# Squares into two buffers in turn, an order re-drawn for each short stretch, products strictly in order

## The chip, the cores and the metric

One Trainium2 chip, of which the kernel uses one core. The metric is the device time of one execution in microseconds (us): 1184.61 us, the median of three runs (1183.17 to 1184.68). The profile is a further execution, which took 1182.92 us.

## The reference, cut to what matters

`x` has 4 batches of 12608 tokens of 128 numbers; `inducing` has 32 points.

```
scale = 1/sqrt(128)
mab(q, kv): a = softmax(scale * q @ kv.T);  return a @ kv
h = mab(inducing, x)            # per batch: 32 points look at 12608 tokens ("p1")
x = mab(x, h)                   # each token looks at the 32 points       ("p2")
h = x @ w_in                    # 128 -> 1024
e = exp(h - max(h));  sm = e / sum(e)
solu = h * sm
ln = (solu - mean(solu)) / sqrt(var(solu) + 1e-6) * g_ln
out = ln @ w_out                # 1024 -> 128
```

All of it is fp32. The variance needs the sum of the squares of each row of 1024; only that sum is used, the squares themselves are not.

## The kernel before, in words

Tokens go in tiles of 128 rows, 99 to a batch, 396 in all; four tiles are a group, 25 groups to a batch. `p1` (L598) and `combine` (L903) make the 32 points of a batch, `p2` (L949) the weights of its tokens; both run ahead of the tiles that need them. The bulk is one pipeline per tile:

- `main` (L1198), `mm1` (L1219), tensor engine (PE): `h` of one tile, 128x1024, into PSUM (line L1233).
- `soft` (L1266), vector engine (DVE): scales it and takes its extreme (L1275); scalar engine (ACT): exp, with the sum of the row read out behind it (L1286); GpSimd (POOL): `e = h * e` (L1290).
- `square` (L1299), ACT: squares `e` with the sum of the row (L1301). The squares are written to one buffer, `sq` (L320), which nothing reads; the sum goes to `G["qe"]`.
- DVE again: a transpose of `e` in 32x32 blocks into the group's buffer `vt` (L1317), of which there are three.
- `products` (L1455), PE: when the four tiles of a group are turned, 32 steps of 32-row products for each half of the array (`w` = 0, 1), L1473. They are put on a list `stream[w]`, from which `beats` (L1146) takes one step at a time: beside a tile's `mm1`, beside turns of `p1` and `p2`, or alone (`driver`, L1174).
- `evacuate` (L1491) copies three groups' products out of PSUM by ACT or DVE (L1501); `finish` (L1513) works out the variances with small steps that go between ACT and POOL (L1526 to L1540) and scales the rows (L1547 on POOL, L1551 on ACT); `stored` (L1556) sends them out on the queue of SP.

The order of instructions on each engine is fixed when the program is built, by `Planner.run` (L237). It keeps a clock for each engine, gives every operation the price written beside it (1208 for L1275, 1133 for L1286, 2330 for L1290, 1040 for L1301, 1163 for L1317, in ns) and a delay from engine to engine (`AFTER`, L95), and takes, on the engine that is free first, the operation of the lowest priority number among those that are ready within a slack (400 ns on ACT, 100 on DVE and POOL, L85):

```
limit = max(clock[eng], first[1]) + self.slack[eng]
pick = min(
    (o for o in self.ops if o[0].eng == eng and o[1] <= limit),
    key=lambda o: (o[2][1] if o[0].prio is None else o[0].prio, o[3]),
)
```

Priorities count in tiles: an operation of tile t has t plus an offset, -8 for the exp, -4 for POOL's multiply and for the square, +2 for L1275, +12 for the transpose (L76 to L83). DMA issues are operations of the engine SP and are picked in the same way.

The chip itself keeps the order and waits by semaphores for what an instruction reads and overwrites. The plan doesn't price a wait between two squares; the build does put one there, as both write `sq`.

Of the kernel before, what the change touches and what calls it, by code (L numbers as in the profile page):

```python
# [10 lines left out]
BF16 = mybir.dt.bfloat16  # L11
U32 = mybir.dt.uint32
I32 = mybir.dt.int32
AF = mybir.ActivationFunctionType
# [5 lines left out]
P = 128  # L20
C = 128
M = 32
FF = 1024
# [7 lines left out]
JB = FF // M  # L31
# [7 lines left out]
NR_POOL = 0  # L39
OS_LATE = 2000  # L40
SLOTS = 3
PIECE = 4
TOKENS = 4
TURN_ON = 90
# [37 lines left out]
PR_SQ = -4  # L82
# [59 lines left out]
class Planner:  # L142
# [94 lines left out]
    def run(self):  # L237
        clock = self.clock
        while self.ops:
            first = min(self.ops, key=lambda o: (max(clock[o[0].eng], o[1]), o[3]))  # L240
            eng = first[0].eng
            limit = max(clock[eng], first[1]) + self.slack[eng]
            pick = min(
                (o for o in self.ops if o[0].eng == eng and o[1] <= limit),
                key=lambda o: (o[2][1] if o[0].prio is None else o[0].prio, o[3]),
            )
            self.ops = [o for o in self.ops if o[3] != pick[3]]
            op, ready, task = pick[:3]
            start = max(clock[eng], ready)
            if eng == "PE" and start - clock[eng] > FILL:  # L250
                self._fill(start - SPARE)
            self.now = start
            op.fn()
            end = start + (self._pe(start, op.cost) if eng == "PE" else op.cost)
            clock[eng] = end
            if eng == "SP":
                end = self.data = max(end + DMA_LAG, self.data) + op.moves / DMA_RATE
            done = Done(eng, end)
            self._step(task, done)
        assert not self.blocked, "the plan is stuck"  # L260
# [3 lines left out]
def set_attention_then_solu_kernel(ctx: ExitStack, tc: tile.TileContext, x, inducing, w_in, w_out, g_ln, out):  # L264
    nc = tc.nc
    NB, N, _ = x.shape
    scale = 1.0 / float(C) ** 0.5
# [24 lines left out]
    plan = Planner(SLACK)  # L292
    spawn, give = plan.spawn, plan.give

    def buf(shape, name, dtype=F32, where=None):
        return (where or const).tile(shape, dtype, name=name)

    def bufs(n, shape, name, dtype=F32):
        return [buf(shape, f"{name}{i}", dtype) for i in range(n)]
# [17 lines left out]
    where = bank_pool.__enter__()  # L317
    bank_e = [buf([P, 512], f"bank_e{i}", where=where) for i in range(8)]
    hn_b = bufs(3, [P, FF], "hn")
    sq = buf([P, FF], "sq", BF16)  # L320

    eu_b = buf([P, EUS, FF], "eu")
    xT_b = buf([C, PG, P], "xT")
# [781 lines left out]
    order, fins = [], []  # L1105
# [18 lines left out]
    for b in range(NB):  # L1124
        for js in fins[b]:
            js = list(js)
            while js:
# [2 lines left out]
                    slot_of[b, j] = (i, j == same[-1])  # L1130
                js = js[len(same) :]

    stream = [[], []]
    flow = {"idle": Event(), "left": 2 * NB * NG - 2, "half": False, "took": 0}

# [38 lines left out]
    def driver():  # L1174

        while flow["left"]:
            mine = [p for q in stream for p in q if p["j"] < JB]
            if not mine:
                flow["idle"] = Event()
                yield flow["idle"]  # L1180
                continue
            op = Op("PE", BEAT * JC, None, Done("PE", min(p["ready"] for p in mine)), prio=min(p["prio"] for p in mine))

            def step():
                beats(JC)
                op.cost = flow["took"]

            op.fn = step
            d = yield op
            closing(d)  # L1190
# [7 lines left out]
    def main():  # L1198
        t = 0
        for b in range(NB):  # L1200
            for j in order[b]:
                left = list(range(ff_groups[j][1]))
                spawn(open_group(b, j), t)
                while left:
                    for item in starts.get(t, ()):
                        spawn(*item)
                    near = left[:WINDOW_TILES]
                    rel = []
                    for s in near:
                        d = yield aT_ready[(b, ff_groups[j][0] + s)]  # L1210
                        rel += d
                    d = yield hw_ready[b]
                    rel += d
                    _, turn = yield TURN
                    hp, hrel = yield H.at(t + H_LAST)
                    op = Op("PE", 4 * BEAT, None, rel, hrel, prio=t - 50)
                    chosen = []

                    def mm1():  # L1219
                        def slot(s):  # L1220
                            return part_of[b, ff_groups[j][0] + s][1]

                        s = min(near, key=lambda s: (load(slot(s) % 2), s))
                        chosen.append(s)
                        ka, i = part_of[b, ff_groups[j][0] + s]
                        aT, hs = aT_of[(b, ka)]["aT"][0], hT[b][1]
                        r = i % 2 * 2

                        def whole(c):
                            for k in range(2 if c == 0 else 0):  # L1230
                                rows = slice((r + k) * M, (r + k + 1) * M)
                                cols = slice(k * 512, (k + 1) * 512)
                                nc.tensor.matmul(hp[:, cols], lhsT=aT[rows, i // 2, :], rhs=hs[rows, cols], start=True, stop=True)  # L1233

                        beats(4, (1 - i % 2,), whole)
                        op.cost = flow["took"]

                    op.fn = mm1
                    d = yield op
                    closing(d)  # L1240
                    s = chosen[0]
                    left.remove(s)
                    if not left and j == order[b][-1]:
                        give(HW, hT[b], d)
                    spawn(soft(t, b, j, s, hp, d), t)
                    t += 1
# [19 lines left out]
    def soft(t, b, j, s, hp, d):  # L1266
        G = grp[(b, j)]
        ka, i = part_of[b, ff_groups[j][0] + s]
        A = aT_of[(b, ka)]
        hn, rel = yield HN  # L1270
        nm, mrel = yield NM
        rn = A["aT"][1][:, i : i + 1]
        d = yield Op(
            "DVE", 1208,
            lambda: nc.vector.tensor_scalar(out=hn, in0=hp, scalar1=rn, scalar2=None, op0=ALU.mult, op1=ALU.min, accum_out=nm),  # L1275
            d, rel, mrel, prio=t + PR_HN,
        )
        give(H, hp, d)
        give(TURN, None, d)
        A["left"] -= 1  # L1280
        if not A["left"]:
            give(AT, A["aT"], d)
        srel = yield G["st"]
        e, rel = yield EU
        de = yield Op(
            "ACT", 1133, lambda: nc.scalar.activation(e, hn, AF.Exp, bias=nm, scale=-1.0, accum_out=G["qe"][:, s, 1:2]), d, rel, srel,  # L1286
            prio=t + PR_EX,
        )
        give(NM, nm, de)
        d = yield Op("POOL", 2330, lambda: nc.gpsimd.tensor_tensor(out=e, in0=hn, in1=e, op=ALU.mult), de, prio=t + PR_MU)  # L1290
        give(HN, hn, d)
        left = []

        def over(d):
            left.append(d)
            if len(left) == 2:
                give(EU, e, *left)

        def square():  # L1299
            ds = yield Op(  # L1300
                "ACT", 1040, lambda: nc.scalar.activation(sq, e, AF.Square, scale=1.0 / 32.0, accum_out=G["qe"][:, s, 0:1]), d,  # L1301
                prio=t + PR_SQ,
            )
            G["squared"].append(ds)
            over(ds)
            if (b, j) != final and len(G["squared"]) == ff_groups[j][1]:
                yield from floor(b, j)

        spawn(square(), t)
        n = ff_groups[j][1]  # L1310
        rel = yield G["vt"]
        if (b, j) == final:
            yield from straight(t, b, j, s, e, d, rel, over)
            return
        dt = yield Op(
            "DVE", 1163,
            lambda: nc.vector.transpose(  # L1317
                out=G["vtb"][:, : n * FF].rearrange("p (j s t) -> p j s t", j=M, s=n)[:, :, s, :],
                in_=e.rearrange("p (a f) -> p a f", f=M),
            ),  # L1320
            d, rel, prio=t + PR_TU,
        )
        over(dt)
        G["turned"].append(dt)
        if len(G["turned"]) == n:
            for w in range(2):
                spawn(products(b, j, t, w), t)
# [127 lines left out]
    def products(b, j, t, w):  # L1455

        G = grp[(b, j)]
        n = ff_groups[j][1]
        rows = n * M
        yield PAIR[w].at(t)  # L1460
        slot, last = slot_of[b, j]
        if slot == 0:
# [2 lines left out]
        bank, rel, mine = held[w]  # L1465
# [16 lines left out]

        ready = max(d.end + AFTER[d.eng]["PE"] for a in (G["turned"], rel, wc_ready.after) for d in a if d is not None)
        stream[w].append(dict(j=0, emit=emit, ready=ready, close=close, prio=t + PR_G2))
        if not last:
            give(PAIR[w], None)
        idle = flow["idle"]
# [192 lines left out]
```

## Time and profile before

| | |
|---|---|
| median of three runs | 1184.61 us (1183.17 to 1184.68) |
| the profiled execution | 1182.92 us |
| its span, first to last instruction | 1181.1 us |
| mean granted clock of the tensor engine | 0.994 |
| busy: PE, ACT, DVE, POOL | 1151.1, 1102.6, 1074.8, 1065.6 us |

A row of instructions gives the start in us, the length in us, the engine, the line, the operation, what it writes and reads, and in brackets the idle time before it with what ended it. Busy times are unions: two instructions that overlap count once. The read of an accumulator (ACTIVATION_READ_ACCUMULATOR) is the tail of the instruction above it; the next instruction may start before the tail ends. Windows give busy us of each engine in a stretch with the number of its instructions, the granted clock of the tensor engine, the share of time that the DMA engines moved data, and GB/s. A PE that is busy need not be full: a product by one half of the array counts as busy.

### The profile page before, as it was taken

The page shows a single profiled execution, that of the slowest core. Times are in us where ns is not written, and L with a number is a line of the kernel's source. Part 1 is how long each engine was busy: PE and PEld are TensorE (multiplying, and loading weights), DVE is VectorE, ACT ScalarE, POOL GpSimd, SP SyncE. Part 2 cuts the span into 40 slices and gives each one's busy share as a digit, 9 for nine tenths or more (in the row PEclk, how much of TensorE's full clock was granted, in tenths as well). Part 3 has the DMA queues.
Part 4 walks back from the last instruction along what each step waited for, and adds up shares of the span by engine and source line. Part 5 has one row for each costly group of instructions (what it writes and reads, how often), then busy time and mean ns, then how long its engine had stood idle before and what let it go on. Part 6 is the DMA issues. An engine that isn't in the chain of part 4 may idle for free.

```text
span 1181.1 us, 68196 instructions
## 1 busy us (share of the span) xinstructions
PE 1151.1 (97%) x30636; PEld 1055.0 (89%) x30636; DVE 1074.8 (91%) x1639; ACT 1102.6 (93%) x2191; POOL 1065.6 (90%) x612
## 2 busy tenths in 40 slices
PE   9999999999999999999999999999999999999996
PEld 7669989998889898999899999999988999999996
DVE  6799989898999899999899998999999999999981
ACT  5699899999999999999999999999999999999994
POOL 3399799898999989899899998989999999999994
PEclk9989999999999999999999999999999999999999
DMA  9532342522143433331423433341313131220103
GB/s 340 230 124 76 111 121 71 155 73 49 41 119 86 141 111 107 96 104 33 120 66 94 121 107 120 102 127 45 101 40 84 40 79 34 67 64 5 49 5 87
DMA packets 166884, 110.62 MB, mean 94 GB/s; under 512 B 78112, under 2 KB 131776, under 8 KB 166464
## 3 DMA queue, kind: packets, MB, share of 16 engines
q1 hardware_dynamic: 166592, 106.27, 31.0%
q8 instruction: 239, 3.92, 1.4%
q14 instruction: 53, 0.43, 0.1%
HBM read 53.51 MB, written 52.17 MB: 89 GB/s over the span
## 4 chain that ended last, share of the span: by engine, by line
PE 45%; POOL 23%; ACT 20%; issue 7%; DVE 3%; DMA 2%; SPq 0%; ACTq 0%; POOLq 0%; DVEq 0%
PE h L1473 32%; POOL eu L1290 16%; ACT sq L1301 9%; ACT eu L1286 6%; PE h L1233 4%; POOL spare L1290 3%; POOL spare L1547 3%; ACT spare L1286 1%; ACT xT L666 1%; ACT spare L1501 1%; PE h L850 1%; PE h L655 1%; ACT a L1013 1%; PE bank_e L557 1%; DMA dl<-dd 1%
## 5 line engine op out<-in xcount | busy, mean ns | idle before, releaser
L1473 PEld LDWEIGHTS h<-wc,vt 32*128 32x128 f32 (+1 forms) x25344 | 954.3, 185 | 45.8 <-issue 13.3
L1473 PE MATMUL h<-wc,vt 32*128 32x129 f32 (+1 forms) x25344 | 983.5, 273 | 10.4 <-ACT spare L1501 3.1
L1290 POOL TENSOR_TENSOR eu<-hn,eu 128x1024 f32<-128x1024 f32 x198 | 466.8, 2377 | 28.7 <-ACT eu L1286 27.7
L1233 PE MATMUL h<-hs,aT 32*128 32x512 f32 x1584 | 419.6, 607 | 6.0 <-DVE spare L1275 2.6
L1317 DVE STREAM_TRANSPOSE vt<-eu 128x1024 f32<-128x1024 f32 x327 | 397.7, 1229 | 11.4 <-POOL eu L1290 10.7
L1301 ACT ACTIVATE sq<-eu 128x1024 bf16<-128x1024 f32 x330 | 346.4, 1050 | 11.3 <-POOL eu L1290 6.5
L1290 POOL TENSOR_TENSOR eu<-spare,eu 128x1024 f32<-128x1024 f32 x132 | 311.7, 2379 | 11.2 <-ACT eu L1286 11.1
L1275 DVE TENSOR_SCALAR_CACHE_REDUCE hn<-h,rn 128x1024 f32<-128x1024 f32 x198 | 248.7, 1260 | 20.6 <-PE h L1233 12.2
L1275 DVE TENSOR_SCALAR_CACHE_REDUCE spare<-h,rn 128x1024 f32<-128x1024 f32 x198 | 248.2, 1260 | 20.7 <-PE h L1233 10.0
L1286 ACT ACTIVATE eu<-hn,nm 128x1024 f32<-128x1024 f32 x198 | 225.4, 1139 | 2.9 <-DVE hn L1275 2.7
L1290 POOL TENSOR_TENSOR spare<-spare 128x1024 f32<-128x1024 f32 x66 | 156.9, 2377 | 12.2 <-ACT spare L1286 12.2
L1286 ACT ACTIVATE eu<-spare,nm 128x1024 f32<-128x1024 f32 x132 | 150.4, 1140 | 2.3 <-DVE vt L1317 1.3
L1233 PEld LDWEIGHTS h<-hs,aT 32*128 32x128 f32 x1584 | 124.6, 186 | 27.5 <-DVE spare L1275 8.1
L1317 DVE STREAM_TRANSPOSE vt<-spare 128x1024 f32<-128x1024 f32 x65 | 80.0, 1231 | 2.0 <-POOL spare L1290 1.8
L1547 POOL TENSOR_TENSOR spare<-spare,fin 128x512 f32<-128x512 f32 x79 | 79.8, 1041 | 1.6
L1301 ACT ACTIVATE sq<-spare 128x1024 bf16<-128x1024 f32 x66 | 69.3, 1050 | 6.9 <-POOL spare L1290 5.3
L1286 ACT ACTIVATE spare<-spare,nm 128x1024 f32<-128x1024 f32 x66 | 75.2, 1140 | 0.4 <-DVE spare L1275 0.4
L1301 ACT ACTIVATION_READ_ACCUMULATOR sq<-eu 128x1 f32 x330 | 62.6, 190 | 0.0
L655 PE MATMUL h<-ident,xn 32*128 32x32 f32 x1188 | 53.6, 227 | 0.1
L655 PEld LDWEIGHTS h<-ident,xn 32*128 32x128 f32 x1188 | 51.1, 141 | 1.1 <-issue 0.8
L1501 ACT COPY spare<-h 128x774 f32<-128x774 f32 (+3 forms) x66 | 42.5, 646 | 9.3 <-PE h L1473 7.0
L666 ACT COPY xT<-h 128x1024 f32<-128x1024 f32 (+2 forms) x42 | 37.8, 900 | 1.1 <-PE h L655 1.1
(189 smaller groups left out, 849.6 us busy)
## 6 DMA issues: line engine op xcount, KB each, us to landing
out_dram<-spare SPq DMA_DIRECT2D x95, 256.0 KB, 3.3
xT<-xd SPq DMA_DIRECT2D x93, 256.0 KB, 3.8
xn<-in_x_dram SPq DMA_DIRECT2D x73, 256.0 KB, 3.7
xd<-xT SPq DMA_DIRECT2D x72, 256.0 KB, 2.6
dl<-dd SPq DMA_DIRECT2D x392, 1.0 KB, 2.3
xd<-vt SPq DMA_DIRECT2D x7, 768.0 KB, 10.2
spare<-in_x_dram SPq DMA_DIRECT2D x5, 768.0 KB, 9.3
dd<-qe SPq DMA_DIRECT2D x95, 4.0 KB, 2.1
```

Of the source, the lines that this page charges most:

```text
L557: nc.tensor.transpose(out=bank[:, :P], in_=ident, identity=ident)
L655: nc.tensor.transpose(out=tr[:, k * 512 + s * M : k * 512 + (s + 1) * M], in_=xn[r, s, :], identity=ident[r, r])
L666: lambda: nc.scalar.copy(xT.rearrange("c s (q t) -> c q s t", q=4)[:, 2 * w : 2 * w + 2, :n, :], tr.rearrange("c (k x) -> c k x", k=2)[:, ...
L1233: nc.tensor.matmul(hp[:, cols], lhsT=aT[rows, i // 2, :], rhs=hs[rows, cols], start=True, stop=True)
L1275: lambda: nc.vector.tensor_scalar(out=hn, in0=hp, scalar1=rn, scalar2=None, op0=ALU.mult, op1=ALU.min, accum_out=nm),
L1286: "ACT", 1133, lambda: nc.scalar.activation(e, hn, AF.Exp, bias=nm, scale=-1.0, accum_out=G["qe"][:, s, 1:2]), d, rel, srel,
L1290: d = yield Op("POOL", 2330, lambda: nc.gpsimd.tensor_tensor(out=e, in0=hn, in1=e, op=ALU.mult), de, prio=t + PR_MU)
L1301: "ACT", 1040, lambda: nc.scalar.activation(sq, e, AF.Square, scale=1.0 / 32.0, accum_out=G["qe"][:, s, 0:1]), d,
L1317: lambda: nc.vector.transpose(out=G["vtb"][:, : n * FF].rearrange("p (j s t) -> p j s t", j=M, s=n)[:, :, s, :], in_=e.rearrange("p (a f) ...
L1473: nc.tensor.matmul(op[:rows, a - 2 * w, :], lhsT=vt[q, k, :], rhs=wc[q, k, :], start=(k == 0), stop=(k == JB - 1))
L1501: return lambda: eng(to, at)
L1547: return lambda: eng.tensor_tensor(out=raw, in0=raw, in1=y[:, i0 : i0 + 4].unsqueeze(2).to_broadcast([rows, 4, C]), op=ALU.mult)
```

## The change

`sq` becomes two buffers that the squares write in turn, in the order in which they are planned. A table `JS` has one pair (wide, turn) for each 20 us of the plan's clock; in `Planner.run` a number between -wide/2 and +wide/2, made from the operation's serial number and turn, is added to its priority when it is compared. Wide is 0 in 18 of the 60 entries, 1.5 in 7, 4 in 16, 10 in 8 and 25 in 11. The products of a group are put on the list of their half only after those of the group before it (`began`), and `driver` looks at the first unfinished entry of each list instead of at all. The price of a square is now a name, with the same 1040; the edit in `whole` gives the same range.

```diff
+STRETCH = 20
+SQ_NS = 1040
+JS = [
+    (0, 0), (4, 945), (25, 681), (0, 0), (0, 0), (0, 0), (0, 0), (1.5, 454),
...
+    (25, 718), (0, 0), (0, 0), (0, 0),
+]
...
             limit = max(clock[eng], first[1]) + self.slack[eng]
+            stretch = int(limit / 1000 / STRETCH)
+            wide, turn = JS[stretch] if stretch < len(JS) else (0, 0)
             pick = min(
                 (o for o in self.ops if o[0].eng == eng and o[1] <= limit),
-                key=lambda o: (o[2][1] if o[0].prio is None else o[0].prio, o[3]),
+                key=lambda o: ((o[2][1] if o[0].prio is None else o[0].prio) + wide * ((o[3] * 40503 + turn * 7919) % 1009 / 1009 - 0.5), o[3]),
             )
...
-    sq = buf([P, FF], "sq", BF16)
+    sq_b = bufs(2, [P, FF], "sq", BF16)
+    squares = [0]
...
+    turn_of = {bj: i for i, bj in enumerate((b, j) for b in range(NB) for j in order[b])}
+    began = [[Event() for _ in turn_of] for _ in range(2)]
...
-            mine = [p for q in stream for p in q if p["j"] < JB]
+            mine = [p for q in stream for p in [next((p for p in q if p["j"] < JB), None)] if p]
...
-            ds = yield Op(
-                "ACT", 1040, lambda: nc.scalar.activation(sq, e, AF.Square, scale=1.0 / 32.0, accum_out=G["qe"][:, s, 0:1]), d,
-                prio=t + PR_SQ,
-            )
+            def squared():
+                squares[0] += 1
+                nc.scalar.activation(sq_b[squares[0] % 2], e, AF.Square, scale=1.0 / 32.0, accum_out=G["qe"][:, s, 0:1])
+
+            ds = yield Op("ACT", SQ_NS, squared, d, prio=t + PR_SQ)
...
         rows = n * M
+        if turn_of[b, j]:
+            yield began[w][turn_of[b, j] - 1]
         yield PAIR[w].at(t)
...
         stream[w].append(dict(j=0, emit=emit, ready=ready, close=close, prio=t + PR_G2))
+        plan.set(began[w][turn_of[b, j]])
```

The entries with wide above 0 between 80 and 1140 us are 40 of 53; 18 of these have 10 or 25. From 1140 us on all are 0.

## Rows read from the trace of the kernel before

**Rows 1.** The page: share of the span and instructions of each engine.
```profile
PE 1151.1 (97%) x30636; PEld 1055.0 (89%) x30636; DVE 1074.8 (91%) x1639; ACT 1102.6 (93%) x2191; POOL 1065.6 (90%) x612
```
**Rows 2.** Windows by stage: PE, PEld, DVE, ACT, POOL busy, clock, DMA, GB/s.
```profile
0.00:60.00 60.00, 55.60 (x604) 40.71 (x604) 42.22 (x128) 34.54 (x84) 20.81 (x23) 1.00 0.78 284
...
80.00:1140.00 1060.00, 1045.41 (x29090) 973.86 (x29090) 998.75 (x1461) 1024.11 (x2013) 1001.60 (x560) 1.00 0.30 84
```
**Rows 3.** Waits, 80 to 1140 us: engine, line, waited for: us, times, longest.
```profile
POOL eu L1290 <- ACT eu L1286: 34.1, 36, 2.5
DVE hn L1275 <- PE h L1233: 12.2, 18, 1.5
POOL spare L1290 <- ACT spare L1286: 12.2, 9, 4.3
...
DVE spare L1275 <- PE h L1233: 10.0, 14, 1.3
DVE vt L1317 <- POOL eu L1290: 9.6, 14, 2.0
...
PEld h L1473 <- DVE vt L1317: 7.2, 12, 0.9
```
**Rows 4.** Waits of ACT alone, 80 to 1140 us, first and last of 18.
```profile
ACT sq L1301 <- POOL eu L1290: 4.7, 12, 1.0
...
ACT a L1013 <- POOL s L1006: 0.2, 1, 0.2
```
**Rows 5.** Timeline of ACT: first and last pair of squares from 80 us on, neighbours between.
```profile
85.18 1.06 ACT L1301 ACTIVATE sq<-eu 128x1024 bf16<-128x1024 f32 x1
86.14 0.20 ACT L1301 ACTIVATION_READ_ACCUMULATOR sq<-eu 128x1 f32 x1
86.43 1.06 ACT L1301 ACTIVATE sq<-eu 128x1024 bf16<-128x1024 f32 x1
...
604.24 1.13 ACT L1286 ACTIVATE eu<-hn,nm 128x1024 f32<-128x1024 f32 x1
...
605.37 1.14 ACT L1286 ACTIVATE eu<-hn,nm 128x1024 f32<-128x1024 f32 x1
...
606.50 1.04 ACT L1301 ACTIVATE sq<-spare 128x1024 bf16<-128x1024 f32 x1
...
607.54 0.20 ACT L1529 ACTIVATE fin<-fin 128x20 f32<-128x20 f32 x1
...
1139.81 1.05 ACT L1301 ACTIVATE sq<-eu 128x1024 bf16<-128x1024 f32 x1
...
1141.05 1.06 ACT L1301 ACTIVATE sq<-eu 128x1024 bf16<-128x1024 f32 x1
```
**Rows 6.** Timeline of POOL: neighbours without a wait.
```profile
617.59 2.38 POOL L1290 TENSOR_TENSOR eu<-spare,eu 128x1024 f32<-128x1024 f32 x1
619.92 2.38 POOL L1290 TENSOR_TENSOR spare<-spare 128x1024 f32<-128x1024 f32 x1
```
**Rows 7.** Timeline of DVE: L1275 and the read behind it.
```profile
683.75 1.28 DVE L1275 TENSOR_SCALAR_CACHE_REDUCE hn<-h,rn 128x1024 f32<-128x1024 f32 x1 [0.49 <-PE h L1233]
684.96 0.08 DVE L1275 DVE_READ_ACCUMULATOR hn<-h,rn 128x1 f32 x1
```
**Rows 8.** Windows of 20 us from 80 to 1140, 53 in all: ACT's emptiest and fullest.
```profile
120.00:140.00 20.00, 20.00 (x624) 19.83 (x618) 18.16 (x28) 17.25 (x32) 17.09 (x9) 1.00 0.47 146
220.00:240.00 20.00, 19.87 (x545) 18.45 (x546) 17.68 (x26) 20.00 (x41) 18.99 (x13) 1.00 0.45 134
```
**Rows 9.** Waits of the whole span: the only one of POOL for a load.
```profile
POOL l L833 <- DMA xT<-xd: 4.6, 1, 4.6
```
**Rows 10.** Windows of 4 us around a fall of the clock.
```profile
1112.00:1116.00 4.00, 2.76 (x44) 1.65 (x45) 4.00 (x5) 4.00 (x9) 4.00 (x3) 1.00 0.45 134
1116.00:1120.00 4.00, 4.00 (x83) 4.00 (x79) 4.00 (x7) 4.00 (x9) 4.00 (x3) 0.57 0.10 5
1120.00:1124.00 4.00, 4.00 (x131) 4.00 (x127) 4.00 (x7) 4.00 (x8) 4.00 (x2) 1.00 0.03 6
```

More of the change, by code (lines that the diff above doesn't have):

```diff
@@ L1229, in whole @@
                         def whole(c):
-                            for k in range(2 if c == 0 else 0):
+                            for k in range(0 if c else 2):
                                 rows = slice((r + k) * M, (r + k + 1) * M)
```

6 rows, old and new, of the table JS are left out of this document.

## Prediction

> **What bounds the kernel now.** I read the shares of the engines first. All four are over 90% busy over the span [rows 1], so no single one explains the time, and PE's 97% is no proof that it is the bound, since a product by half the array counts as busy. The windows by stage come next [rows 2]. In the first 60 us DVE, ACT and POOL are loosely filled; the bulk lies between 80 and 1140 us. There ACT is busy 1024.1 of 1060 us, POOL 1001.6, DVE 998.8. ACT is thus 35.9 us short of full, POOL 58.4 and DVE 61.2. The waits of that stretch say who holds whom [rows 3]: POOL sits 34.1 + 12.2 = 46.3 us until ACT's exp, in 45 waits, of the 58.4 that it is idle; DVE sits 22.2 us for PE's `h` and some 10 us for POOL. ACT itself has 18 rows of waits, which add to 26.7 us, the largest 4.7 [rows 4]. So the pipeline is evenly loaded, ACT is the fullest, and the others wait for it more than it for them. What frees time on ACT, or lets it wait less, is worth something; 35.9 us plus what hides inside "busy" is all that there is.
>
> **The squares.** In ACT's timeline two neighbours without a wait follow each other at the price of the first: exp to exp 604.24 to 605.37, 1.13 us; a square to the next instruction 606.50 to 607.54, 1.04 us [rows 5]. The next one starts some 0.1 us before the read of the accumulator ends. Where a square follows a square it doesn't: 85.18 to 86.43 is 1.25 us, and the start comes 0.09 us after the read ended (86.14 + 0.20 = 86.34) [rows 5]. I count 65 such pairs from 80 us to 1140 (70 in all), with a median of 1.23 us from start to start. The extra is 1.23 - 1.04 = 0.19 us, and 65 x 0.19 = 12.4 us, 70 x 0.19 = 13.3 us. It hides from the rows of waits, since about half is overlap lost and the rest is a gap too short to be listed. Two exps in a row also end with an accumulator's read and lose nothing; what the squares have that the exps have not is the common destination `sq`. With two buffers in turn a square overwrites what the last but one wrote, which is over by then. So ACT gains up to 13.3 us, if the number of pairs stays as it is.
>
> How much of it reaches the end? Nothing, if ACT merely waits longer for POOL, DVE or PE; all of it, if ACT ends everything. ACT is 96.6% busy in the bulk, and 46.3 us of POOL's idle time waits for ACT [rows 2, 3]; against that, DVE waits 22.2 us for PE, which an earlier square doesn't help. I take half of 12.4, **6 us**, bounds 0 and 13.3.
>
> [...]
>
> **The order.** The table touches 40 of the 53 stretches between 80 and 1140 us. No instruction is added; it moves instructions on every engine, SP's DMA issues among them. What it can be worth depends on whether the plan's clock is the chip's. Its prices are, where I can check them: L1290 costs 2330 ns in the plan and 619.92 - 617.59 = 2.33 us in the trace [rows 6]; L1275 1208 ns and 684.96 - 683.75 = 1.21 us [rows 7]; exp 1133 ns and 1.13 us; a square alone 1040 ns and 1.04 us [rows 5]. The one price that is off is the pair of squares, which the other part mends. So a stretch that is fuller in the plan should be fuller on the chip, up to the small delays.
>
> How full can a stretch get? Of the 53 windows of 20 us ACT fills 17.25 in the emptiest and 20.00 in the fullest [rows 8]; the mean is 1024.1 / 53 = 19.32, and the 26 fullest have a mean of 19.77. Moving 40 stretches from the mean to that level would give 40 x 0.45 = 18 us. Not all of this can come: what ACT lacks in a window is partly the short gaps between squares, already counted (65 x 0.10 = 6.5 us of the 35.9), and an order that fills one stretch borrows from the next. I take six tenths, **11 us**. Upper end: all of ACT's 26.7 us of waits go [rows 4]. Lower end, a loss: each of the 18 stretches of wide 10 or 25 costs one more wait of POOL for an exp, 46.3 / 45 = 1.03 us [rows 3], 18 x 1.03 = 18.5 us. The forecast lies nearer the upper rows because the plan's prices agree with the trace.
>
> SP's part: loads are issued in another order too. I cost it at nothing, because DMA is busy 0.30 of the bulk [rows 2] and the whole span has one wait of POOL for a load, 4.6 us [rows 9]; each load that loses its cover would cost about that.
>
> **Products in order, and the driver.** No instruction is added. In the plan a group's products now wait until those of the group before are listed. In the order of before the groups come one after the other anyway; where the new order turns a later group first, its products are held, its `vt` buffer (one of three) with them, and behind these DVE's transposes of the group after. The nearest rows are PE's weight loads that wait for a transpose, 7.2 us in 12 waits, 0.6 each [rows 3]: between 0 and 40 x 0.6 = 24 us. I take 0: a late group costs PE something only when its list has run dry, and 12 waits in 1060 us say that this is seldom.
>
> **Sum.** 6 + 11 + 0 = 17 us off the profiled execution's 1182.92: 1165.9. The median of the runs stands 1.7 us above that execution, so the forecast is **1167.5 us**, 1.4% faster. The end is left alone: the stretches from 1140 us are not touched.
>
> **Rivals.**
> *Squares alone.* The order is neither better nor worse on the chip, as waits of a tenth shift. For: most waits here are under 2 us [rows 3], so small errors matter. Against: the prices agree. 1184.6 - 6 = 1178.6.
> [...]
> *Deeper.* Both at their upper ends: 1184.6 - 26.7 - 12.4 = 1145.5. Against: POOL has only 58.4 us and DVE 61.2 to give, and would have to be nearly full too.
> [...]
> *Slower: POOL starved of exps.* The exp of a tile stands 4 before its square. A width of 1.5 or 4 can't turn that round; 10 and 25 can, and then squares (nobody waits for them but a buffer) run before exps for which POOL waits. One such wait in each of the 18 wide stretches is 18.5 us, less 6 for the squares: 1184.6 + 12.5 = 1197. It decides from six extra waits on, if the narrow stretches give nothing. For: 45 such waits exist already. Against: ACT has two or three exps ready in most places, as the pair at 604.24 shows [rows 5].
>
> **How the numbers follow.** Forecast (1158 to 1175) 0.49, squares alone 0.14, the gap stays 0.05, deeper (under 1158) 0.13, clock given back 0.06, slower 0.13. About 0.2%, 2.4 us, is what runs of this kernel can tell from no change. Faster: 0.49 + 0.14 + 0.05 + 0.13 = 0.81; same 0.06; slower 0.13. The range runs from 1150 (half the way into "deeper", some 0.05 left out) to 1190 (which leaves out most of "slower", about 0.09).
>
> **What would show it.** Pairs of squares from start to start at 1.04 us instead of 1.23 show the first step right; 1.23 shows it wrong. ACT busier than 19.5 of 20 us in the mean window, and POOL's waits for exps under 46 us, show the second. [...] Wrong altogether it would be if ACT's idle time grew while the squares closed up: then ACT was not what held the others.

## The result: 1170.88 us, and the profile after

The changed kernel takes 1170.88 us (median of four runs, 1169.65 to 1172.95) against 1184.64 us for the kernel before beside it; the ratio is 0.9885, with an interval from 0.9865 to 0.9905. That is 13.6 us less (0.0115 x 1184.6), and the time stands 3.4 us above the forecast of 1167.5. The profiled execution has a span of 1167.7 us against 1181.1. In a second measurement, beside the last runs below, the ratio was 0.9879 (0.9856 to 0.9902).

The lines of the new code are numbered otherwise: the exp is L1303 (L1286 before), POOL's multiply L1307 (L1290), the square L1319 (L1301), DVE's first step L1292 (L1275), the transpose L1335 (L1317), the products L1493 (L1473), the evacuation L1522 (L1501).

The page's first part after, which answers to [rows 1]:

```profile
PE 1142.5 (98%) x30637; PEld 1050.3 (90%) x30637; DVE 1075.2 (92%) x1635; ACT 1098.7 (94%) x2193; POOL 1065.8 (91%) x614
```

The work is the same but for a few instructions (four fewer on DVE, two more on ACT and on POOL each; DVE and POOL are as busy in us as they were); it stands in a shorter span. ACT's busy time is 3.9 us less: squares in a row now overlap. The window of the bulk, first of the kernel before, then after, from 80 to 1120 us, where both are in full swing (columns as in [rows 2]):

```profile
80.00:1120.00 1040.00, 1025.41 (x28505) 953.92 (x28505) 978.75 (x1435) 1005.07 (x1977) 981.60 (x552) 1.00 0.31 85
```

```profile
80.00:1120.00 1040.00, 1030.88 (x28845) 962.31 (x28840) 994.15 (x1456) 1013.43 (x2001) 992.03 (x555) 1.00 0.31 85
```

In the same 1040 us DVE works 15.4 us more, POOL 10.4 and ACT 8.4, and in work done ACT's share is more than its busy time says, since squares in a row now take less. All three fill up together. The 52 windows of 20 us have a mean of 1013.43 / 52 = 19.49 us of ACT, against 1005.07 / 52 = 19.33.

ACT's timeline after, three squares in a row, to be read beside the first three of [rows 5]:

```profile
89.98 1.07 ACT L1319 ACTIVATE sq<-eu 128x1024 bf16<-128x1024 f32 x1
90.94 0.20 ACT L1319 ACTIVATION_READ_ACCUMULATOR sq<-eu 128x1 f32 x1
91.03 1.05 ACT L1319 ACTIVATE sq<-eu 128x1024 bf16<-128x1024 f32 x1
91.98 0.19 ACT L1319 ACTIVATION_READ_ACCUMULATOR sq<-eu 128x1 f32 x1
92.07 1.05 ACT L1319 ACTIVATE sq<-spare 128x1024 bf16<-128x1024 f32 x1
```

From start to start they are 1.05 and 1.04 us apart, and the second starts 0.11 us before the first one's accumulator read ends (90.94 + 0.20 = 91.14). There are 91 such pairs now, with a median of 1.04 us.

Waits after, 80 to 1140 us, which answer to [rows 3]:

```profile
POOL eu L1307 <- ACT eu L1303: 34.3, 40, 2.8
...
POOL spare L1307 <- ACT spare L1303: 9.3, 8, 2.4
DVE hn L1292 <- PE h L1250: 8.5, 13, 2.2
...
DVE spare L1292 <- PE h L1250: 8.3, 16, 1.1
...
PEld h L1493 <- DVE vt L1335: 4.1, 6, 0.9
```

POOL's waits for exps are 43.6 us instead of 46.3, and DVE's for PE's `h` 16.8 instead of 22.2. ACT's own 18 rows of waits add to 23.4 us instead of 26.7.

### The profile page after: what moved, and what is told of

It reads as the page before. It is cut to its first block, busy times and chain, and to the rows that moved or that the text cites. A ratio compares the mean times of both kernels' runs of the same rounds, so it can differ in the third digit from the quotient of the medians.

```text
span 1167.7 us, 68127 instructions
## 1 busy us (share of the span) xinstructions
PE 1142.5 (98%) x30637; PEld 1050.3 (90%) x30637; DVE 1075.2 (92%) x1635; ACT 1098.7 (94%) x2193; POOL 1065.8 (91%) x614
## 4 chain that ended last, share of the span: by engine, by line
PE 51%; ACT 17%; POOL 16%; DVE 6%; issue 5%; DMA 3%; SPq 1%; ACTq 0%; POOLq 0%; DVEq 0%
PE h L1493 39%; POOL eu L1307 12%; ACT sq L1319 6%; ACT eu L1303 5%; PE h L1250 4%; POOL spare L1307 3%; DVE vt L1335 2%; DVE spare L1292 2%; ACT spare L1303 1%; ACT spare L1522 1%; DVE hn L1292 1%; DMA spare<-in_x_dram 1%; POOL spare L1568 1%; PE h L670 1%; DMA dl<-dd 1%
## 5 line engine op out<-in xcount | busy, mean ns | idle before, releaser
L1493 PEld LDWEIGHTS h<-wc,vt 32*128 32x128 f32 (+1 forms) x25344 | 953.1, 185 | 40.7 <-issue 14.4
L1493 PE MATMUL h<-wc,vt 32*128 32x129 f32 (+1 forms) x25344 | 979.3, 273 | 7.3 <-ACT spare L1522 3.7
L1307 POOL TENSOR_TENSOR eu<-hn,eu 128x1024 f32<-128x1024 f32 x170 | 403.3, 2383 | 21.9 <-ACT eu L1303 21.5
L1335 DVE STREAM_TRANSPOSE vt<-eu 128x1024 f32<-128x1024 f32 x326 | 397.4, 1229 | 3.6 <-POOL eu L1307 3.3
L1307 POOL TENSOR_TENSOR eu<-spare,eu 128x1024 f32<-128x1024 f32 x159 | 377.1, 2384 | 20.4 <-ACT eu L1303 20.3
L1319 ACT ACTIVATE sq<-eu 128x1024 bf16<-128x1024 f32 x329 | 344.6, 1048 | 7.1 <-POOL eu L1307 6.3
L1292 DVE TENSOR_SCALAR_CACHE_REDUCE hn<-h,rn 128x1024 f32<-128x1024 f32 x199 | 249.8, 1262 | 18.3 <-PE h L1250 10.3
L1292 DVE TENSOR_SCALAR_CACHE_REDUCE spare<-h,rn 128x1024 f32<-128x1024 f32 x197 | 247.7, 1261 | 15.5 <-PE h L1250 8.5
L1303 ACT ACTIVATE eu<-hn,nm 128x1024 f32<-128x1024 f32 x170 | 193.9, 1142 | 4.6 <-DVE hn L1292 4.4
L1303 ACT ACTIVATE eu<-spare,nm 128x1024 f32<-128x1024 f32 x159 | 181.3, 1141 | 3.1 <-DVE spare L1292 2.9
L1250 PEld LDWEIGHTS h<-hs,aT 32*128 32x128 f32 x1584 | 127.7, 186 | 20.3 <-DVE hn L1292 4.7
L1307 POOL TENSOR_TENSOR spare<-spare 128x1024 f32<-128x1024 f32 x38 | 90.6, 2384 | 3.4 <-ACT spare L1303 3.3
L1335 DVE STREAM_TRANSPOSE vt<-spare 128x1024 f32<-128x1024 f32 x66 | 81.0, 1228 | 3.4 <-POOL spare L1307 3.3
L1307 POOL TENSOR_TENSOR spare<-hn,spare 128x1024 f32<-128x1024 f32 x29 | 69.1, 2384 | 5.9 <-ACT spare L1303 5.9
L1319 ACT ACTIVATE sq<-spare 128x1024 bf16<-128x1024 f32 x67 | 70.2, 1047 | 1.0 <-POOL spare L1307 1.0
L1319 ACT ACTIVATION_READ_ACCUMULATOR sq<-eu 128x1 f32 x329 | 62.8, 191 | 0.0
L1522 ACT COPY spare<-h 128x774 f32<-128x774 f32 (+3 forms) x69 | 43.8, 636 | 10.1 <-PE h L1493 7.6
L1303 ACT ACTIVATE spare<-spare,nm 128x1024 f32<-128x1024 f32 x38 | 43.3, 1141 | 0.3 <-DVE spare L1292 0.3
```

The source lines that it names most:

```text
L1319: nc.scalar.activation(sq_b[squares[0] % 2], e, AF.Square, scale=1.0 / 32.0, accum_out=G["qe"][:, s, 0:1])
L1335: lambda: nc.vector.transpose(out=G["vtb"][:, : n * FF].rearrange("p (j s t) -> p j s t", j=M, s=n)[:, :, s, :], in_=e.rearrange("p (a f) ...
L1493: nc.tensor.matmul(op[:rows, a - 2 * w, :], lhsT=vt[q, k, :], rhs=wc[q, k, :], start=(k == 0), stop=(k == JB - 1))
L1522: return lambda: eng(to, at)
```

## The experiments

Ratios are to the kernel before, run in the same rounds.

**The two buffers alone.** The instructions of every engine stand in the order of before.

```diff
-    sq = buf([P, FF], "sq", BF16)
+    sq_b = bufs(2, [P, FF], "sq", BF16)
...
-nc.scalar.activation(sq, e, AF.Square, ...)
+nc.scalar.activation(sq_b[squares[0] % 2], e, AF.Square, ...)
```

> The kernel before with the two buffers for the squares alone; its instructions stand in the same order. My theory (the gap is the buffer's, half of it reaches the end): squares that follow each other start 1.04 us apart instead of 1.23, 65 pairs of the bulk give ACT 12.4 us, and the time falls by about 6 us, to 1178.6 (ratio 0.995; 0.989 if all of it reaches the end). [...] Rival, ACT only waits longer elsewhere: pairs at 1.04 us, ratio 1.000, and ACT's waits grow by about 12 us.

Measured: ratio 0.9968 (0.9950 to 0.9985), so 3.8 us of gain, with 1.8 to 5.9 in the interval. Its timeline of ACT:

```profile
86.78 1.07 ACT L1303 ACTIVATE sq<-eu 128x1024 bf16<-128x1024 f32 x1
87.73 0.20 ACT L1303 ACTIVATION_READ_ACCUMULATOR sq<-eu 128x1 f32 x1
87.83 1.05 ACT L1303 ACTIVATE sq<-eu 128x1024 bf16<-128x1024 f32 x1
```

The gap is the buffer's: 70 pairs as before, with a median of 1.04 us instead of 1.23. But most of the saving did not reach the end. The first rows of its waits from 80 to 1140 us:

```profile
ACT sq L1303 <- POOL eu L1291: 6.0, 17, 1.0
ACT sq L1303 <- POOL spare L1291: 4.5, 5, 1.4
```

The squares wait 10.5 us for POOL (L1291 there), where in the kernel before ACT's largest row was 4.7 us [rows 4], and all of ACT's rows together are 31.1 us instead of 26.7. So 4.4 of the 12.4 us saved turned into waits that the profile lists, and the rival by which ACT only waits longer holds for that part. The start differs too: from 60 to 80 us the granted clock is 0.57, where it was 0.83 before, and ACT is one tile behind by 80 us (last section):

```profile
60.00:80.00 20.00, 18.90 (x166) 9.03 (x164) 18.17 (x26) 18.07 (x33) 15.74 (x9) 0.57 0.29 94
```

By 600 us and by 1120 us this run is one tile ahead of the kernel before (386 and 770 of ACT's instructions of the exp's line, two to a tile, against 384 and 768), so between 80 and 1120 us it won two tiles, some 5.4 us at 2.7 us a tile (520 us for 192 tiles). That is one execution of each kernel. The times themselves go with the clock from one execution to the next: of the 17 executions of the kernel before beside these runs the fastest, 1180.73 us, had a mean granted clock of 0.995, the slowest, 1190.32 us, one of 0.985. The medians are 0.989 there and 0.991 for the two buffers; how much of the 3.8 us came by way of the clock no run separates.

**One buffer in the changed kernel**, which leaves the order and the rest.

```diff
-nc.scalar.activation(sq_b[squares[0] % 2], e, AF.Square, ...)
+nc.scalar.activation(sq_b[0], e, AF.Square, ...)
```

> The changed kernel with one buffer for the squares; order and everything else as in the changed kernel. The changed kernel has 91 pairs of squares, so with the gap of 0.19 us back ACT loses 17 us. My theory (about half reaches the end): 1170.9 + 8.5 = 1179 us, ratio 0.996 to before: the order alone would be worth some 5 us. Rival, the order carries the gain and the buffers nothing: 1171, ratio 0.9885. Rival, the order makes pairs of squares and so is worth something only with two buffers: 1185 or more, ratio 1.000.

Measured: ratio 0.9940 (0.9920 to 0.9960), 7.1 us less than before. The three squares of the fence above stand there thus:

```profile
89.75 1.07 ACT L1319 ACTIVATE sq<-eu 128x1024 bf16<-128x1024 f32 x1
90.71 0.20 ACT L1319 ACTIVATION_READ_ACCUMULATOR sq<-eu 128x1 f32 x1
91.00 1.06 ACT L1319 ACTIVATE sq<-eu 128x1024 bf16<-128x1024 f32 x1
91.96 0.19 ACT L1319 ACTIVATION_READ_ACCUMULATOR sq<-eu 128x1 f32 x1
92.24 1.06 ACT L1319 ACTIVATE sq<-spare 128x1024 bf16<-128x1024 f32 x1
```

The gap is back at 1.25 and 1.24 us, in an order that has 91 pairs instead of 70. The order alone is thus worth 7.1 us, even with 17 us of such gaps in it, and the second buffer in this order 0.9940 - 0.9885 = 0.0055, or 6.5 us, against 3.8 in the old order. As each ratio can be off by 0.002, the 6.5 stand for some 3 to 10 us (an estimate), so the two worths of the buffer are not told apart. Neither rival holds: the order doesn't carry everything, and it isn't worthless without the buffers. The theory's 0.996 lies at the edge of the interval.

**Another draw.** The table's widths with every turn moved on by 500.

```diff
+JS = [(w, (t + 500) % 1009) for w, t in JS]
```

> The changed kernel with the same widths, but every turn moved on by 500, so each stretch gets another draw of the same kind that nobody chose. Theory that the choice is what matters: an unchosen order is worse than none, as in the slower rival of the prediction; POOL's waits for exps grow by some 18 us or more and the time goes past that of before, 1190 to 1220 us (ratio above 1.005). Rival, any shuffle of ties is as good: 1171, ratio 0.9885. Rival, the order does nothing and the buffers carry the gain: about 1178, ratio 0.995.

Measured: ratio 1.0407 (1.0379 to 1.0436), 48 us slower than before. Windows by stage and the first wait from 80 to 1130 us:

```profile
80.00:600.00 520.00, 499.23 (x13610) 456.30 (x13610) 469.97 (x716) 479.62 (x939) 458.19 (x254) 0.99 0.32 92
600.00:1120.00 520.00, 507.17 (x13937) 470.46 (x13934) 485.27 (x689) 494.82 (x971) 488.13 (x275) 1.00 0.28 76
```

```profile
POOL eu L1308 <- ACT eu L1304: 70.8, 52, 6.8
```

With the row of the other buffer (11.6 us) POOL waits 82.4 us for exps, and ACT is busy 479.6 + 494.8 = 974.4 of the 1040 us in which it was busy 1005.1 before. So ACT as a whole was not short of time. Its own rows of waits add to 61.3 us (26.7 before), the largest that of squares for POOL (4.7 us before [rows 4]):

```profile
ACT sq L1320 <- POOL eu L1308: 14.7, 31, 1.2
```

This is the slower rival of the prediction, and it comes true for an order that nobody chose: this shuffle is harmful, and the same widths are a gain or a loss by which draws stand in the table.

**Narrow and wide draws.** The same unchosen turns, with one width throughout.

```diff
+JS = [(1.5 if w else 0, (t + 500) % 1009) for w, t in JS]
```

> The changed kernel with width 1.5 in each stretch that has a width above 0, and the unchosen turns of the run before (each moved on by 500). Theory of the prediction's slower rival: a width below 4 can't put a square before the exp of the same tile, so this order is about as good as none: ratio about that of the two buffers alone, 0.997, and POOL's waits for exps stay near 46 us. Rival, any order that nobody chose costs time, since also ties between tiles and between DVE's operations turn: ratio 1.005 or more, with DVE's and ACT's waits grown rather than POOL's.

```diff
+JS = [(25 if w else 0, (t + 500) % 1009) for w, t in JS]
```

> The changed kernel with width 25 in each stretch that has a width above 0, and the same unchosen turns. Theory (wide numbers turn exps, squares and transposes round): worse than the mixed unchosen draw, which stood at ratio 1.041, because all 42 stretches are wide instead of 19; if the loss goes with the wide stretches, 0.041 x 42 / 19 = 0.09, so a ratio near 1.09, and POOL's waits for exps above 82 us. Rival, the width doesn't matter, only that nobody chose: ratio near 1.04.

Measured: narrow 1.0169 (1.0129 to 1.0208), wide 1.0655 (1.0616 to 1.0694). The first waits of the narrow one, then its window, then the window of the wide one:

```profile
POOL eu L1308 <- ACT eu L1304: 50.4, 43, 5.3
POOL spare L1308 <- ACT spare L1304: 18.3, 13, 5.4
```

```profile
80.00:600.00 520.00, 509.58 (x13782) 468.19 (x13778) 473.66 (x717) 485.83 (x952) 464.75 (x258) 0.98 0.32 93
```

```profile
80.00:600.00 520.00, 499.51 (x13037) 451.36 (x13036) 452.95 (x687) 464.93 (x902) 435.78 (x239) 0.96 0.31 89
```

The narrow draw was expected to be harmless and is not: POOL waits 68.7 us for exps, ACT's rows of waits from 80 to 1140 us add to 47.0 us (26.7 before) and DVE's to 74.8 (58.1), and PE's mean clock is 0.98 of full from 80 to 600 us, which in the kernel before rounds to 1.00 for the whole bulk [rows 2]. The wide one is worse still (POOL's waits for exps 106.4 us, clock 0.96), but by 0.066 and not by the 0.09 that a loss in step with the number of wide stretches would give. The theory of the narrow draw is thus refuted; its rival has the time right (above 1.005) and not the sign, since POOL's waits grew beside ACT's and DVE's. The theory of the wide draw has the direction right and the size wrong. What holds is that each of the three unchosen orders cost time, the wider one more; all three have one set of turns, so how much another set would cost is not shown.

**The first half of the table**, to 580 us.

```diff
+JS = JS[:29]
```

> The changed kernel with the first 29 entries of the table, to 580 us; from there the order is made with no number added. Theory that the order's gain is gathered evenly, stretch by stretch: about half of the order's part is lost, 1170.9 + 3.5 = 1174 us (ratio 0.991). Rival, the gain is that of the end (how the last tiles fall): all of the order's part lost, about 1178 (0.995). Rival, the gain is that of a few early stretches: 1171 (0.9885).

Measured: ratio 0.9926 (0.9907 to 0.9945). From the two buffers alone (0.9968) to the whole change (0.9885) the order is worth 0.0083; half the table keeps 0.0042 of it. ACT's exps, with the reads of their sums, counted from the start, in the kernel before, then in the change, then with half the table:

```profile
0.00:600.00 600.00, 233.38 (x384) 0.99 0.38 114
0.00:1120.00 1120.00, 466.91 (x768) 1.00 0.33 96
```

```profile
0.00:600.00 600.00, 236.09 (x390) 0.99 0.37 114
0.00:1120.00 1120.00, 469.98 (x776) 0.99 0.33 96
```

```profile
0.00:600.00 600.00, 236.52 (x391) 1.00 0.38 114
0.00:1120.00 1120.00, 469.20 (x773) 1.00 0.33 96
```

Two instructions are one tile. At 600 us both tables lead the kernel before by about three tiles; by 1120 us the whole table leads by four and half of it by two and a half. One tile of each lead is there with the two buffers alone (386 and 770). The gain is gathered along the way, not at the end, and by these counts more of it before 600 us than behind. That the lead shrinks without the table is a matter of one tile and may be chance.

**A new table.** The plan was let choose again: per stretch the draw of 150 with which it has done the most work 30 us after the stretch.

```diff
-JS = [(0, 0), (4, 945), (25, 681), (0, 0), ...]
+JS = [(0, 0), (25, 903), (25, 359), (10, 539), ...]
```

> The changed kernel with another table, chosen afresh by the plan: for each stretch that one of 150 draws (wide 0, 1.5, 4, 10 or 25) with which the plan has done the most work 30 us after the stretch ends. Theory that an order chosen by the plan's own clock is also the better one on the chip, because its prices are the chip's: faster than the two buffers alone (ratio 0.997), somewhere from 0.986 to 0.993. Rival, the table of the change suits this chip by luck: 0.997 or above, and up to the 1.017 to 1.066 of the unchosen draws.

> The changed kernel as it is, on the chip and in the rounds of the new table: ratio 0.9885 as before, between 0.9865 and 0.9905.

Measured: the new table 0.9934 (0.9910 to 0.9958), the change again 0.9879 (0.9856 to 0.9902). The new table stands a hair outside the range that was expected and, by its middle, ahead of the two buffers alone (0.9968), though the intervals overlap (0.9950 to 0.9958). So this freshly chosen table is on the right side of the unchosen ones by more than 0.02, and as far as one table can show it the plan's choice carries over to the chip; that it beats no table at all is likely and not settled. How the table of the change itself was chosen is not known here. No run beat the change itself.

**Products in order.** This was not run by itself, because it has nothing to show: taken out of the changed kernel, the wait for `began` leaves the list of instructions of all five engines as it is, and so does `driver`'s edit; with an empty table the new code gives the order of before.

## Why the prediction was right, and where its sizes were off

*What bounds the kernel.* Right: no engine alone. One reading was off and changes no term: DVE's waits for POOL are five rows with 21.6 us together, not some 10. In the run with two buffers ACT was freed and then waited 4.4 us longer by the rows. Its whole idle time from 80 to 1140 us stayed at 35.6 us (35.9 before): what the short gaps gave up, waits took. The sign for "wrong altogether", idle time that grows while the squares close up, was thus not met, but not by much. In the change DVE and POOL won more than ACT.

*The squares.* The mechanism is right and measured from both sides: 1.23 us with one buffer, 1.04 with two, in either order. The size: 0.19 x 65 = 12.4 us of ACT was right, and half of it, 6 us, was taken to reach the end. Alone it was 3.8 us (1.8 to 5.9), in the new order 6.5 of 91 x 0.19 = 17.3 us. So about a third by the middle values; half lies just outside the interval of the first and inside that of the second.

With the destinations apart, squares follow each other without a gap, at 1.04 us from start to start, the second 0.11 us before the first one's accumulator read ends. Of ACT's instructions on a whole tile only squares into one buffer have a regular gap: in the kernel before, an exp behind an exp starts after 1.13 us, the median of 64 pairs without a listed wait. Between the small steps of `finish`, which write `fin` one after another (L1533 to L1535), there is a shorter one, 0.03 us, the median of 40 there.

*The order.* "I take six tenths, 11 us" measured 7.1 us with one buffer, which is too little even at the upper end of the interval (9.5), and 0.9968 - 0.9885 = 0.0083, or 9.8 us, on top of two, where 11 lies within the noise. The term was reckoned as if 40 stretches gained 0.27 us each, six tenths of the way from 19.32 to 19.77, which is 11 / 53 = 0.21 for each window of the bulk; the mean window rose by 0.16 (19.49 against 19.33), and that is with the squares in it. "Busier than 19.5" was thus just missed, while POOL's waits under 46 us came (43.6). That six tenths came out near is in part luck: nothing in the working gives this share rather than another. The reason for a gain at all, that the plan's prices are the chip's, fits the new table, which the plan chose (0.9934), against the three unchosen ones (1.017 to 1.066); no run changed a price to test it.

*Products in order.* 0, as forecast: PE's weight loads wait 4.1 us for transposes, 7.2 before.

*The sum.* 17 us forecast, 13.6 measured. Alone the two parts are 3.8 + 7.1 = 10.9, together 13.6. That they help each other has a reason that the trace shows, as the new order has more squares in a row (91 pairs against 70), which one buffer makes dear and two make free, and the prediction added the terms with the pairs of the old order. But the 2.7 us between 10.9 and 13.6 are within the noise of the three ratios.

*The rivals.* "Squares alone" is refuted by the order's 7.1 us, "the gap stays", 0.05 in the chances, by pairs at 1.04 us. "Slower: POOL starved of exps" did not occur in the change (43.6 us of such waits against 46.3), but it comes with the same widths and other turns: 82.4 us, beside longer waits of ACT itself. Its limit was wrong, though: "a width of 1.5 or 4 can't turn that round" looked only at an exp and the square of its own tile. With offsets of -8 and -4, the exp of tile t has the same priority as the square of tile t - 4, and a tie is turned by any width. That this is what cost the narrow draw its 20 us is argued from the code; no run separates it from other ties. "Clock given back", 0.06 in the chances, by which a lower granted clock takes the gain again, did not decide here: 0.74 from 60 to 80 us (0.83 before) and one fall near 1096 us, as before near 1116 [rows 10]; two unchosen draws show a lower clock, 0.98 and 0.96 over 520 us. The fall after:

```profile
1088.00:1092.00 4.00, 3.55 (x60) 2.41 (x52) 4.00 (x6) 3.25 (x8) 4.00 (x4) 1.00 0.10 2
1092.00:1096.00 4.00, 2.25 (x44) 2.28 (x48) 4.00 (x7) 4.00 (x7) 4.00 (x3) 0.89 0.02 4
1096.00:1100.00 4.00, 4.00 (x96) 4.00 (x94) 4.00 (x5) 4.00 (x9) 4.00 (x2) 0.69 0.00 0
```

PE was busy 3.55 and then 2.25 of 4 us. The granted clock is 0.89 in the second of these windows and 0.69 in the next, where PE is full again; from 1100 to 1104 us it is 1.00. Whether PE's idle time brought the fall was not tried. In ten runs of this kernel the mean granted clock lies between 0.989 and 0.995, so the order alone does not fix how much the clock falls.

## What to carry to other kernels

A buffer that is written and never read can still hold up its writers (here 1.23 us from square to square with one buffer, 1.04 with two): look at the distance from start to start of two like instructions in a row, not at the rows of waits, and give the junk two places in turn. Three orders from one random set of turns cost 2 to 7% in this evenly loaded pipeline. Of two chosen tables one gained 0.8% over the two buffers alone, the other, chosen by a plan whose prices agree with the trace, perhaps 0.3%. So before trusting a searched order, compare the plan's prices with the trace, and run an unchosen draw beside the chosen one. Measure two edits apart and together, and ask how far the noise lets the parts be added: here the order made more pairs of squares, of which only the second buffer takes the gap, and the runs could not yet tell 10.9 us from 13.6.

## What was not expected of the hardware

The start is not the same from one execution to the next, in one and the same order: from 60 to 80 us the granted clock was 0.83 in the kernel before and 0.57 in the run with two buffers, which has its order; it was 0.74 after, and 0.91 with the first half of the table, which has the same instructions in the same order up to 580 us of the plan. In the run with two buffers ACT had begun 18 instructions of the exp's line by 80 us, and 20 before, so one tile was lost there and won back later:

```profile
0.00:80.00 80.00, 10.79 (x18) 0.89 0.66 237
```

Whether the lower clock made that tile late, or what was late there lowered the clock, was not tried.
